# Softmax sums and reciprocals turned on VectorE instead of TensorE, and other begins for the blocks of powers

## The chip, the cores and the metric

The kernel runs on one core of a Trainium2 chip. The metric is device time in microseconds (us), the median of several executions; lower is better. TensorE is PE in the profile (PEld its weight loads), VectorE DVE, ScalarE ACT, GpSimd POOL, and SyncE, which issues most DMAs, SP.

## The reference

Two heads are computed and concatenated along the last axis. All data is float32, L = 2048, D = 448.

```
# A: a convolution with a state-space kernel (S4D), 448 channels, 256 states
dt = exp(log_dt);  A = -exp(log_A_real) + 1j*A_imag;  C = (C_real + 1j*C_imag)*dt
P  = exp(A*dt * pos)                       # (448, 256, 2048): powers of one number per channel and state
K  = 2*real(einsum("dn,dnl->dl", C, P))
y  = irfft(rfft(u, 2L)*rfft(K, 2L))[:L] + u*D_skip
# B: full attention, 16 heads of 28
q, k, v = heads(x @ wqkv);  p = softmax(q k^T * 28**-0.5);  out = (p v) @ wo
```

## The kernel before

One program does both heads, interleaved by hand. A first stage (to about 230 us) projects x to q, k and v and makes the seeds of the powers. Then comes the attention loop, and beside it, in slots, everything of head A.

**The attention loop** (lines 1061-1118) has 256 steps: 16 units u (4 groups g of 4 heads, times 4 chunks c of 512 queries), each of 16 steps over 128 keys. A step issues its work in the order written out in ORDER (line 35): four scores matmuls s0-s3 (s_mm, line 769: PE writes pss, ACT takes the exponential into p), four matmuls m0-m3 for the row maxima of the unit after next to come (max_mm, line 189: PE writes a bank of the ring pm; for m0 ACT takes a relu into rl, for m1 DVE adds and reduces with a custom instruction, for m2 and m3 DVE reduces), the product with v (pv, pv_step, line 776: eight column-tiled matmuls into po), up to three power products on DVE (v: vec, line 1056), the planning of blocks of powers (k), and two slots (f). After step 236 there are no more maxima, and a step has a third slot. In this part of the program every engine keeps the order in which the program issues (KEPT, line 89), so an instruction that waits holds up all that stands behind it on its engine.

**The ring.** w_tile (line 127) hands out three PSUM banks pm0-pm2 in turn. The maxima's matmuls and all slot work use it; a matmul into a bank waits until the last reader of that bank is done.

**Slots.** slot (line 1012) runs at most one thing: first what is urgent and due (soon_slot, line 1005: kept with a number of the slot from which it is due), then output projections (p_due), then matmuls of the powers (m_due), then u parts (u_due), then spectrum and finish tasks of head A (f_slot). UG (line 41) says after how many slots the maxima's end, the sums and the scaling are due. After the last step a loop (line 1122) runs slots until all is done.

**The end of a unit** (fin, line 789). The product with v has v's 28 columns and a column of ones for each head in 32 partitions, so po holds for each of four heads 28 rows of output and in row 28 the sum of the softmax. fin copies po to o (ACT). Two slots later *sums* takes a ring bank and multiplies, with o as the weights, by a constant sel (one column per head that picks row 28): 16 small products, in 32 instructions, whose output has queries on partitions. DVE takes the reciprocal of these 16 columns, ACT spreads each over 32 columns (rb). Another two slots later *scale* multiplies rb by the identity, again in 32 instructions, so that each reciprocal stands in the 32 rows of its head, and DVE multiplies o by that (on). on goes to DRAM, or, for the last group, into four output projections (project, line 815), each due from two steps after fin on, one more for each step.

**Blocks of powers.** 56 blocks b of eight channels. A block's e half (nine POOL instructions, e_power, line 689) and g half (DVE, g_powers, line 703) are begun by k_begin (line 1032); before that k_seed (line 1027) has made its two seeds, one per step, in tiles with two buffers each:

```python
def k_seed(s_):
    b = k_due[0] if k_due else NB
    if b < NB and b not in egs and done["mm"] >= b - 2 and K0 + b * KP <= s_ + (1 if b in es else 2):
        k_seeds(b)
```

KP is 3.5: block b is not begun before step 3.5 b. Its matmuls (k_mm, line 730) are due in slots KD = 4, 5 and 6 steps after the begin: two products of e and g, the second of which sets done["mm"] = b, and a fold with w. k_start (line 685) copies the factors into PSUM (zg) on ACT at the begin.

**Head A besides.** u parts (lines 622-667) run in steps 3 to about 102; spectrum tasks (line 831) from step 195 on, finish tasks (line 874) from about 233 on; the first finish job also loads the constant wb (line 895).

Of the kernel before, what the change touches and what calls it, by code (L numbers as in the profile page):

```python
# [8 lines left out]
F32 = mybir.dt.float32  # L9
F32R = mybir.dt.float32r  # L10
I32 = mybir.dt.int32
AF = mybir.ActivationFunctionType
# [6 lines left out]
D = 448  # L19

H = 16
DH = 28
G = 4
HG = H // G
CQ = 512
NQ = L // CQ
NK = L // 128
# [13 lines left out]
UG = (2, 2, 4)  # L41
PS = 1
SGB, XB, XL = 2, 5, 4
K0, KP, KD, UP = 0, 3.5, 4, 3
A0, A1 = 26, 31

N1 = 32
N2 = 64
# [3 lines left out]
NB = D // 8  # L52
# [40 lines left out]
def body(ctx, tc, a, out):  # L93
    nc = Engines(tc)
# [22 lines left out]
    const = pool(ctx, "const")  # L117
    ident = const.tile([128, 128], F32, name="ident")
    nc.sync.dma_start(ident, a["ident"])
    sel = const.tile([128, HG], F32, name="sel")  # L120
    kones = const.tile([128, 1], F32, name="kones")
    w1 = const.tile([128, 2, 128], F32, name="w1")

# [3 lines left out]
    def w_tile():  # L127

        n_ring[0] += 1
        return ps_w[0].tile([128, CQ], F32, name=f"pm{n_ring[0] % ps_w[1]}")  # L130
# [7 lines left out]
    def mm32(o, w, x_, start, stop, at=0):  # L138

        for i in range(w.shape[-1] // 32):  # L140
            c = slice(32 * i, 32 * i + 32)
            nc.tensor.matmul(o[c], w[:, c], x_, start=start, stop=stop, tile_position=(0, at + 32 * i))
# [85 lines left out]
    with ExitStack() as st:  # L228
# [32 lines left out]
        t = a["A_log_dt"]  # L261
# [56 lines left out]
        pw2 = s_p.tile([128, LV], F32, name="pw2")  # L318
        nc.sync.dma_start(pw2, a["pw2"])
        nc.sync.dma_start(kones, a["kones"])  # L320
        nc.sync.dma_start(sel, a["sel"])
        nc.sync.dma_start(w1, a["w1"])
        def split_w(s):
            for k in range(NCK):
# [285 lines left out]
    kq_p = pool(kq_st, "kq_p")  # L610
# [58 lines left out]
    sds, egs = {}, {}  # L669
# [58 lines left out]
    uts, zgs, es = {}, {}, {}  # L728
# [60 lines left out]
    def fin(u, s_):  # L789
        g, c = divmod(u, NQ)  # L790
        o = kq_p.tile([128, CQ], F32, name="o")
        nc.scalar.activation(o, o_u[u], AF.Copy)
        on = kq_p.tile([128, CQ], F32, name="on", bufs=2)
        rb = kq_p.tile([128, 4, HG, 32], F32, name="rb")
        og = og_u.pop(u, None)

        def sums():
            pw = w_tile()
            for t in range(4):
                mm32(pw[:, t * HG:(t + 1) * HG], o[:, t * 128:(t + 1) * 128], sel, start=True, stop=True)  # L800
            r = kq_p.tile([128, 4, HG], F32, name="r", bufs=2)
            nc.vector.reciprocal(r, pw[:, :4 * HG].rearrange("p (t h) -> p t h", h=HG))
            nc.scalar.activation(rb, r[:, :, :, None].to_broadcast([128, 4, HG, 32]), AF.Copy)

        def scale():
            pw = w_tile()
            for t in range(4):
                mm32(pw[:, t * 128:(t + 1) * 128], rb[:, t].rearrange("p h e -> p (h e)"), ident, True, True)
            nc.vector.tensor_tensor(on, o, pw, ALU.mult)
            if g < G - 1:  # L810
                nc.sync.dma_start(on_d[c][g], on)
            else:
                p_due.extend((s_ + PD + PS * t, lambda t=t: project(t)) for t in range(4))

        def project(t):
            pw = w_tile()
            ts = slice(t * 128, (t + 1) * 128)
            for g2 in range(G):
                mm32(pw[:, :D], og[:, g2, ts] if g2 < G - 1 else on[:, ts], wo_t[g2 // 2][:, g2 % 2, :],
                     start=g2 == 0, stop=g2 == G - 1)  # L820
            y = kq_p.tile([128, D], F32, name="y", bufs=2)
            nc.scalar.activation(y, pw[:, :D], AF.Copy)
            q0 = c * CQ + t * 128
            nc.sync.dma_start(out[q0:q0 + 128, D:], y)

        soon_slot(UG[1], sums)
        soon_slot(UG[2], scale)

    fk = {}

# [43 lines left out]
    def finish(f, qc, p, ps, bufs=(2, 2)):  # L874

        t_ = {}

        def rows(t, m, i, n):

            w = t.ap[0][0]  # L880
            return bass.AP(tensor=t.tensor, offset=t.offset + (16 * m + 4 * qc + i) * w + f * DF,
                           ap=[[32 * w, 64], [w, n], [1, DF]])

        def load():
            t_["zi"] = p.tile([128, 4, 2, DF], F32, name="zi", bufs=bufs[0])
            nc.sync.dma_start(t_["zi"], z_d[f].rearrange("(q m h c) k d -> (h c k) q m d", m=2, h=2, c=2)
                              [:, qc * 4:qc * 4 + 4])
            t_["u"] = p.tile([128, 4, DF], F32, name="ut", bufs=2)
            for m in range(2):
                nc.sync.dma_start(t_["u"][64 * m:64 * m + 64], rows(u_a, m, 0, 4))  # L890
            if "dsk" not in fk:
                fk["dsk"], fk["wb"] = p.tile([128, D], F32, name="dsk"), p.tile([128, 64], F32, name="wb")
                t = a["A_D_skip"]
                nc.sync.dma_start(fk["dsk"], bass.AP(tensor=t.tensor, offset=t.offset, ap=[[0, 128], [1, D]]))
                nc.sync.dma_start(fk["wb"], a["wb"])

        def skip():
            nc.gpsimd.tensor_tensor(t_["u"], t_["u"],
                                    fk["dsk"][:, None, f * DF:(f + 1) * DF].to_broadcast([128, 4, DF]), ALU.mult)

        def one(i):
            if i == 0:
                t_["ot"] = p.tile([128, 4, DF], F32, name="ot", bufs=bufs[1])
            pf = ps()[:, :DF]
            for m in range(2):
                mm32(pf[64 * m:64 * m + 64, :], fk["wb"], t_["zi"][:, i, m, :], True, True, 64 * m)
            ot = t_["ot"]
            jbi = lambda t, o_: t.rearrange(o_ + " -> p j b i", j=4, i=2)
            nc.vector.tensor_tensor(jbi(ot[:, i], "p (j b i)"), jbi(pf, "p (b j i)"), jbi(t_["u"][:, i], "p (j b i)"), ALU.add)
            if i % 2:  # L910
                for m in range(2):
                    nc.sync.dma_start(rows(out, m, i - 1, 2), ot[64 * m:64 * m + 64, i - 1:i + 1])
        return load, [(0, lambda i=i: one(i)) for i in range(4)], skip
# [11 lines left out]
    k_seeds(0)  # L925
    k_seeds(0)

    urgent, back = collections.deque(), collections.deque()
    powers = {"g": collections.deque(), "e": collections.deque()}
    done = {"mm": -1}  # L930
    u_jobs = [u_stage1(q) for q in range(16)] + [u_stage2(m) for m in range(16)]
# [17 lines left out]
    u_due = collections.deque((3 + UP * i + (UP / 2) * c + (4 if i > 15 else 0), i, c) for i in range(32) for c in range(2))  # L949
    k_due = collections.deque(range(NB))  # L950
    m_due = collections.deque()
# [3 lines left out]
    f_tasks = {k: collections.deque() for k in "sf"}  # L955
    f_loaded = {k: collections.deque() for k in "sf"}
    s_done = [0]
    n_slot, f_next = [0], {"s": 0, "f": 0}
# [46 lines left out]
    def soon_slot(gap, f):  # L1005
        n_urgent[0] += 1
        urgent.append((n_slot[0] + gap, n_urgent[0], f))
        q = sorted(urgent)
        urgent.clear()
        urgent.extend(q)  # L1010

    def slot(s_):
        n_slot[0] += 1
        if urgent and urgent[0][0] <= n_slot[0]:
            urgent.popleft()[2]()
        elif s_ >= NS and f_slot(s_, "s"):
            pass
        elif p_due and p_due[0][0] <= s_:
            p_due.popleft()[1]()
        elif m_due and m_due[0][0] <= s_:  # L1020
            m_due.popleft()[1]()
        elif u_due and u_due[0][0] <= s_:
            u_part(*u_due.popleft()[1:])
        else:
            f_slot(s_, "s") or f_slot(s_, "f")

    def k_seed(s_):
        b = k_due[0] if k_due else NB
        if b < NB and b not in egs and done["mm"] >= b - 2 and K0 + b * KP <= s_ + (1 if b in es else 2):
            k_seeds(b)  # L1030

    def k_begin(s_):
        if not (k_due and K0 + k_due[0] * KP <= s_ and k_due[0] in egs and not powers["e"] and not powers["g"]):
            return
        b = k_due.popleft()
        k_start(b)
        powers["g"] += g_powers(b)
        powers["e"] += [lambda i=i, q=q: e_power(b, i, q) for i in range(3) for q in range(3)]
        p0, p1, p2 = k_mm(b)

        def m1():
            p1()
            done["mm"] = b
        m_due.extend((s_ + KD + i, t_) for i, t_ in enumerate((p0, m1, p2)))
        last[0] = b
# [73 lines left out]
    pv_step(*prev)  # L1119
    fin(prev[0], NS)  # L1120
    s = NS
    while urgent or p_due or m_due or u_due or any(q[k] for q in (f_jobs, f_tasks, f_loaded) for k in "sf"):
        slot(s)
        s += 0.5
    assert not k_due and not powers["g"] and not powers["e"]
# [4 lines left out]
def constants():  # L1130
    import numpy as np
    k = {}
    k["ident"] = np.eye(128)
    sel, ones = np.zeros((128, HG)), np.zeros((128, 1))
    for j in range(HG):
        sel[32 * j + DH, j] = 1.0
        ones[32 * j + DH:32 * j + DH + 2] = 1.0
    k["sel"], k["kones"] = sel, ones
    k["pw2"] = np.tile(2.0 ** np.arange(LV), (128, 1))
    n1, k1 = np.arange(N1), np.arange(N1)  # L1140
    n2, k2 = np.arange(N2), np.arange(N2)
# [43 lines left out]
```

## Time and profile before

| what | time |
|---|---|
| median of 3 runs | 1278.66 us (1276.97 to 1278.9) |
| the profiled execution | 1278.83 us |
| its span, first to last instruction | 1277.0 us |
| PE busy | 1216.2 us (95%) |
| ACT busy | 967.0 us (76%) |
| DVE busy | 922.6 us (72%) |
| POOL busy | 843.6 us (66%) |

A row of the profile that begins with L77 names line 77, the helper through which every instruction is issued, so groups are told apart by their tiles, written out<-in. After the tiles come the shapes, the count, then the busy time in us and the mean of one in ns, then the engine's idle time before them with what ended it. A row of a stretch is its begin and end, its length, then the busy time of each engine with the number of its instructions, the granted clock of PE, the DMA engines' busy share and GB/s. A row of the timeline is start, length, engine, instruction, and idle time before it in brackets. Ends of matmuls are modelled, so several of them overlap in the rows; what a piece of PE's work costs is better read from the starts of what follows, or from whole steps.

### The profile page before, as it was taken

Reading aid. Unit: us, or ns where it says so; the run is one execution under the profiler, and the core shown is the slowest. Engines: PE = TensorE matmul, PEld = TensorE weight load, DVE = VectorE, ACT = ScalarE, POOL = GpSimd, SP = SyncE. Lnnn points to the kernel's source line nnn. Section 1 sums busy time; section 2 is a strip of 40 time slices with the busy share of each in tenths; the row PEclk is TensorE's granted clock in tenths of the full one; section 3 lists DMA queues with packets and bytes.
Section 4 is the critical chain, followed back from the end, with each engine's and each line's share of the span. In section 5 each row is a group of like instructions: output and inputs, shape, how many; then the busy total and the mean of one; then the engine's idle time right before and its main releaser. Section 6 shows DMA issues by size and latency. Waiting matters only on the chain.

```text
span 1277.0 us, 33251 instructions
## 1 busy us (share of the span) xinstructions
PE 1216.2 (95%) x12593; PEld 692.5 (54%) x12593; DVE 922.6 (72%) x2106; ACT 967.0 (76%) x2162; POOL 843.6 (66%) x728
## 2 busy tenths in 40 slices
PE   6788888999999999999999999999999999999998
PEld 4666764555555555555555555555555555544433
DVE  5788966877777877778778988888887645645111
ACT  5888865788888888888888888888887656656552
POOL 2666740798788888878689999989995222324321
PEclk9999898899999999999999999999999999999999
DMA  6678789436554645475533133432224533657656
GB/s 194 211 258 290 275 278 359 124 88 187 159 154 114 169 118 159 123 224 177 171 101 96 57 80 105 145 91 71 83 60 149 171 139 135 205 162 237 203 163 174
DMA packets 203528, 206.22 MB, mean 161 GB/s; under 512 B 98344, under 2 KB 162408, under 8 KB 201320
## 3 DMA queue, kind: packets, MB, share of 16 engines
q1 hardware_dynamic: 202840, 203.50, 51.8%
q8 instruction: 99, 1.62, 0.5%
q10 hardware_dynamic: 528, 0.59, 0.2%
q14 instruction: 61, 0.50, 0.1%
HBM read 121.60 MB, written 82.18 MB: 160 GB/s over the span
## 4 chain that ended last, share of the span: by engine, by line
PE 79%; DVE 9%; ACT 5%; issue 3%; POOL 2%; DMA 1%; SPq 1%; ACTq 0%; POOLq 0%; DVEq 0%
PE pm L77 44%; PE pss L77 17%; PE po L77 17%; DVE tri L77 1%; ACT tri L77 1%; DVE mx L77 1%; DVE sg L77 1%; SPq L77 1%; ACT rl L77 1%; DVE hl L77 1%; DVE px L77 1%; ACT p L77 1%; PE pt L77 1%; POOL p L77 1%; DVE g L77 1%
## 5 line engine op out<-in xcount | busy, mean ns | idle before, releaser
L77 ACT ACTIVATE p<-pss 128x512 f32<-128x512 f32 x1024 | 561.3, 611 | 111.5 <-PE pss L77 108.4
L77 PE MATMUL pss<-qhat,khat 128*128 128x512 f32 x1024 | 402.8, 399 | 1.5 <-ACT p L77 1.4
L77 DVE TENSOR_REDUCE mx<-pm 128x1 f32<-128x512 f32 x480 | 308.3, 683 | 108.9 <-PE pm L77 106.8
L77 PE MATMUL pm<-khat,qhat 128*128 128x512 f32 x749 | 326.3, 439 | 6.6 <-ACT rl L77 4.4
L77 POOL TENSOR_TENSOR e<-e,sdb 128x256 f32<-128x256 f32 x168 | 201.8, 1201 | 111.4 <-ACT e L77 62.2
L77 PE MATMUL po<-p,v 128*32 128x512 f32 x2048 | 269.1, 594 | 0.0
L77 POOL TENSOR_TENSOR e<-e,eu 128x256 f32<-128x256 f32 x168 | 248.1, 1477 | 13.2
L77 PEld LDWEIGHTS pm<-khat,qhat 128*128 128x128 f32 x749 | 141.2, 189 | 202.8 <-ACT p L77 46.9
L77 DVE CUSTOM_DVE_ANT_0 rl<-pm,rl 128x512 f32<-128x512 f32 x259 | 178.2, 688 | 73.7 <-ACT rl L77 70.8
L77 PEld LDWEIGHTS pss<-qhat,khat 128*128 128x128 f32 x1024 | 190.4, 188 | 46.1 <-issue 10.8
L77 POOL TENSOR_TENSOR eu<-e,sdb 128x256 f32<-128x256 f32 x168 | 201.9, 1202 | 0.0
L77 POOL TENSOR_TENSOR p<-pr,pr 64x448 f32<-64x448 f32 x64 | 73.1, 1142 | 161.4 <-PE pm L77 134.7
L77 ACT ACTIVATE rl<-pm 128x512 f32<-128x512 f32 x259 | 156.8, 607 | 15.4 <-PE pm L77 9.4
L77 DVE TENSOR_TENSOR g<-g,zg 128x128 f32<-128x128 f32 x392 | 161.9, 413 | 3.4
L77 PE MATMUL pm<-kdif,qhat 128*128 128x512 f32 x249 | 100.9, 405 | 6.0 <-DVE xn L77 4.1
L77 PE MATMUL pm<-xh,khat 128*128 128x512 f32 x256 | 85.0, 423 | 12.1 <-DVE hl L77 5.3
L77 DVE TENSOR_TENSOR zg<-g,zg 128x128 f32<-128x128 f32 x224 | 88.0, 393 | 5.0
L77 PEld LDWEIGHTS pm<-e,g 128*32 128x32 f32 x3584 | 57.2, 109 | 43.9 <-issue 16.2
L77 DVE TENSOR_TENSOR pr<-pm,ub 128x448 f32<-128x448 f32 x64 | 37.0, 619 | 56.4 <-PE pm L77 42.0
L77 PE MATMUL pm<-e,g 128*32 128x64 f32 x3584 | 73.0, 222 | 1.9 <-POOL e L77 1.3
L77 ACT ACTIVATE y<-pm 128x448 f32<-128x448 f32 x48 | 26.5, 553 | 58.2 <-PE pm L77 35.9
L77 ACT ACTIVATE ub<-pm 128x224 f32<-128x224 f32 (+1 forms) x96 | 38.7, 448 | 39.5 <-PE pm L77 37.4
(135 smaller groups left out, 1436.7 us busy)
## 6 DMA issues: line engine op xcount, KB each, us to landing
sdb<-sd SPq DMA_DIRECT2D x55, 336.0 KB
qhat<-q SPq DMA_DIRECT2D x64, 256.0 KB
khat<-k SPq DMA_DIRECT2D x64, 256.0 KB
sd<-sg SPq DMA_DIRECT2D x8, 1456.0 KB
k<-hl SPq DMA_DIRECT2D x16, 512.0 KB
mw<-in_mw SPq DMA_DIRECT2D x16, 512.0 KB
sd<-qhat SPq DMA_DIRECT2D x8, 896.0 KB
yu_d<-ub SPq DMA_DIRECT2D x64, 112.0 KB
```

The lines of the kernel that those rows point to most:

```text
L77: i = f(*args, **kw)
```

## The change

The sums' and the scaling's matmuls go, and with them sel and ACT's spreading copy. *sums* now turns o on DVE in blocks of 32x32 (SBUF to SBUF, 128x512), so that column 28 of each block holds the sums with queries on partitions; DVE takes the reciprocal of these 16 columns. *scale* turns the reciprocals, each read 32 times, into a ring bank, again on DVE, and multiplies as before. Both leave the slots: they stand in a queue of their own, *free*, with the same number of slots to wait, and slot runs whatever of it is due and then one thing as before. The condition of k_seed and k_begin on the step is now a table K_BEGIN: 10/3 steps per block up to block 33, then 3.75 from step 113.5 on; the rest of both conditions is as it was. The constant wb is loaded at the start, in sel's place, and no longer by the first finish job.

```diff
-K0, KP, KD, UP = 0, 3.5, 4, 3
+KD, UP = 4, 3
+K_BEGIN = [b * 10 / 3 if b < 34 else 112 + (b - 33.6) * 3.75 for b in range(56)]
...
-    sel = const.tile([128, HG], F32, name="sel")
+    wb = const.tile([128, N2], F32, name="wb")
...
         on = kq_p.tile([128, CQ], F32, name="on", bufs=2)
-        rb = kq_p.tile([128, 4, HG, 32], F32, name="rb")
         og = og_u.pop(u, None)
+        t_ = {}
 
         def sums():
-            pw = w_tile()
-            for t in range(4):
-                mm32(pw[:, t * HG:(t + 1) * HG], o[:, t * 128:(t + 1) * 128], sel, start=True, stop=True)
-            r = kq_p.tile([128, 4, HG], F32, name="r", bufs=2)
-            nc.vector.reciprocal(r, pw[:, :4 * HG].rearrange("p (t h) -> p t h", h=HG))
-            nc.scalar.activation(rb, r[:, :, :, None].to_broadcast([128, 4, HG, 32]), AF.Copy)
+            t = kq_p.tile([128, NK, 32], F32, name="rb")
+            nc.vector.transpose(t.rearrange("p b e -> p (b e)"), o)
+            t_["r"] = kq_p.tile([128, NK], F32, name="r", bufs=2)
+            nc.vector.reciprocal(t_["r"], t[:, :, DH])
 
         def scale():
             pw = w_tile()
-            for t in range(4):
-                mm32(pw[:, t * 128:(t + 1) * 128], rb[:, t].rearrange("p h e -> p (h e)"), ident, True, True)
+            nc.vector.transpose(pw.rearrange("p (b e) -> p b e", e=32), t_["r"][:, :, None].to_broadcast([128, NK, 32]))
             nc.vector.tensor_tensor(on, o, pw, ALU.mult)
...
-        soon_slot(UG[1], sums)
-        soon_slot(UG[2], scale)
+        free.append((n_slot[0] + UG[1], sums))
+        free.append((n_slot[0] + UG[2], scale))
...
     def slot(s_):
         n_slot[0] += 1
+        while free and free[0][0] <= n_slot[0]:
+            free.popleft()[1]()
         if urgent and urgent[0][0] <= n_slot[0]:
...
-        if b < NB and b not in egs and done["mm"] >= b - 2 and K0 + b * KP <= s_ + (1 if b in es else 2):
+        if b < NB and b not in egs and done["mm"] >= b - 2 and K_BEGIN[b] <= s_ + (1 if b in es else 2):
...
-        if not (k_due and K0 + k_due[0] * KP <= s_ and k_due[0] in egs and not powers["e"] and not powers["g"]):
+        if not (k_due and K_BEGIN[k_due[0]] <= s_ and k_due[0] in egs and not powers["e"] and not powers["g"]):
```

More of the change, by code (lines that the diff above doesn't have):

```diff
@@ L320, in body @@
         nc.sync.dma_start(kones, a["kones"])
-        nc.sync.dma_start(sel, a["sel"])
+        nc.sync.dma_start(wb, a["wb"])
         nc.sync.dma_start(w1, a["w1"])
@@ L891, in load @@
             if "dsk" not in fk:
-                fk["dsk"], fk["wb"] = p.tile([128, D], F32, name="dsk"), p.tile([128, 64], F32, name="wb")
+                fk["dsk"] = p.tile([128, D], F32, name="dsk")
                 t = a["A_D_skip"]
                 nc.sync.dma_start(fk["dsk"], bass.AP(tensor=t.tensor, offset=t.offset, ap=[[0, 128], [1, D]]))
-                nc.sync.dma_start(fk["wb"], a["wb"])
         def skip():
@@ L905, in one @@
             for m in range(2):
-                mm32(pf[64 * m:64 * m + 64, :], fk["wb"], t_["zi"][:, i, m, :], True, True, 64 * m)
+                mm32(pf[64 * m:64 * m + 64, :], wb, t_["zi"][:, i, m, :], True, True, 64 * m)
             ot = t_["ot"]
@@ L926, in body @@
     k_seeds(0)
-    urgent, back = collections.deque(), collections.deque()
+    urgent, free = collections.deque(), collections.deque()
     powers = {"g": collections.deque(), "e": collections.deque()}
@@ L1121, in body @@
     s = NS
-    while urgent or p_due or m_due or u_due or any(q[k] for q in (f_jobs, f_tasks, f_loaded) for k in "sf"):
+    while urgent or free or p_due or m_due or u_due or any(q[k] for q in (f_jobs, f_tasks, f_loaded) for k in "sf"):
         slot(s)
@@ L1133, in constants @@
     k["ident"] = np.eye(128)
-    sel, ones = np.zeros((128, HG)), np.zeros((128, 1))
+    ones = np.zeros((128, 1))
     for j in range(HG):
-        sel[32 * j + DH, j] = 1.0
         ones[32 * j + DH:32 * j + DH + 2] = 1.0
-    k["sel"], k["kones"] = sel, ones
+    k["kones"] = ones
     k["pw2"] = np.tile(2.0 ** np.arange(LV), (128, 1))
```

## The prediction

> **What bounds the kernel now.** I read the page first: the span, then the chain that ended last.
>
> ```profile
> span 1277.0 us, 33251 instructions
> ...
> PE 79%; DVE 9%; ACT 5%; issue 3%; POOL 2%; DMA 1%; SPq 1%; ACTq 0%; POOLq 0%; DVEq 0%
> PE pm L77 44%; PE pss L77 17%; PE po L77 17%; DVE tri L77 1%; ACT tri L77 1%; DVE mx L77 1%; DVE sg L77 1%; SPq L77 1%; ACT rl L77 1%; DVE hl L77 1%; DVE px L77 1%; ACT p L77 1%; PE pt L77 1%; POOL p L77 1%; DVE g L77 1%
> ```
>
> The chain is PE, above all PE writing pm, the ring of three banks. Next I cut the attention at the first scores matmul (pss) of a step: steps 0-100 (with the u jobs), 101-192 (powers only), 193-236, and from 237.
>
> ```profile
> core 0: us, PE busy (x) PEld busy (x) DVE busy (x) ACT busy (x) POOL busy (x), PEclk, DMA share, GB/s
> 230.54:634.07 403.53, 402.04 (x4728) 219.59 (x4726) 317.29 (x751) 337.12 (x779) 333.44 (x261) 1.00 0.53 151
> 634.07:963.69 329.62, 326.67 (x3904) 185.86 (x3902) 286.51 (x686) 278.55 (x632) 303.63 (x241) 1.00 0.31 86
> 963.69:1167.55 203.86, 203.05 (x2099) 108.16 (x2097) 121.66 (x253) 132.72 (x263) 65.21 (x53) 1.00 0.52 171
> 1167.55:1277.03 109.48, 99.21 (x1118) 40.66 (x1116) 22.35 (x51) 52.86 (x100) 32.13 (x24) 0.99 0.64 189
> ```
>
> PE is busy almost all of the first three stretches, at a granted clock of 1.00. The reader should look at the third busy column too: DVE has 86 us free in the first stretch (403.5 less 317.3), but only 43 in the second (87% busy). POOL, 92% busy there, has the powers' e half; it bounds nothing as long as the steps there don't get shorter, and by the sum below they don't. So what leaves PE is worth its full time only where DVE can take what it gets. Single steps show what PE's pieces cost:
>
> ```profile
> 899.99:903.02 3.03, 3.03 (x17) 1.58 (x16) 2.71 (x7) 2.44 (x7) 2.87 (x3) 1.00 0.93 229
> 842.90:846.39 3.49, 3.49 (x49) 2.02 (x48) 3.39 (x10) 2.97 (x8) 3.41 (x3) 1.00 0.00 0
> 625.58:629.82 4.24, 4.24 (x57) 2.28 (x56) 3.42 (x10) 3.37 (x9) 3.54 (x3) 1.00 0.62 221
> 849.86:853.18 3.32, 3.32 (x49) 1.85 (x48) 2.99 (x9) 3.04 (x8) 3.16 (x3) 1.00 0.49 106
> 682.15:686.52 4.37, 4.37 (x81) 3.05 (x80) 3.84 (x9) 3.08 (x8) 4.29 (x3) 1.00 0.18 67
> 735.26:739.37 4.11, 4.04 (x65) 2.29 (x64) 3.52 (x10) 3.83 (x9) 3.95 (x5) 1.00 0.02 4
> 294.27:298.40 4.13, 4.03 (x66) 2.29 (x65) 3.55 (x10) 3.84 (x9) 3.91 (x5) 1.00 0.15 62
> 616.57:620.90 4.33, 4.01 (x65) 2.29 (x64) 3.91 (x10) 3.78 (x9) 4.09 (x6) 1.00 0.88 284
> ```
>
> In order: a step with empty slots 3.03 us; with one product of the powers (e,g) 3.49, so a product is 0.46; with product and u part 4.24, so a u part is 0.75; with the sums alone 3.32, so **the sums are 0.29**; with the spread of the reciprocals and a product 4.37, so **the spread is 0.88**. In the last three the sums stand beside a fold of powers, which I take as a product: parts of 3.78, so they hold 0.33, 0.35 and 0.55 of waiting, 1.2 in all. PE is a sum of parts.
>
> **The change, part by part.** The groups with shapes kept apart give what goes and what stays:
>
> ```profile
> L77 PE MATMUL pm<-ident,rb 128*32 128x128 f32 x512 | 17.3, 275 | 0.6 <-ACT rb L77 0.6
> L77 PE MATMUL pm<-sel,o 128*32 128x4 f32 x512 | 7.0, 175 | 0.3 <-ACT o L77 0.3
> L77 ACT ACTIVATE rb<-r 128x512 f32<-128x512 f32 x16 | 10.1, 630 | 4.9 <-DVE r L77 4.9
> L77 DVE RECIPROCAL r<-pm 128x16 f32<-128x16 f32 x16 | 4.0, 251 | 0.3 <-PE pm L77 0.3
> L77 DVE TENSOR_TENSOR on<-o,pm 128x512 f32<-128x512 f32 x16 | 10.9, 682 | 2.3 <-PE pm L77 2.1
> L77 DVE TENSOR_TENSOR g<-g,zg 128x256 f32<-128x256 f32 x224 | 92.3, 412 | 1.5
> L77 DVE TENSOR_TENSOR g<-g,zg 128x512 f32<-128x512 f32 x56 | 38.2, 681 | 0.0
> ```
>
> *Off PE:* per unit 32 sums and 32 spread instructions (512/16 each), 0.29 + 0.88 = 1.17 us; 16 units. *Off ACT:* 0.63 per unit, not on the chain; I cost it at nothing. *On to DVE:* two turns of 128x512 per unit. No row shows a turn. From 256 to 512 columns a g product goes from 412 to 681 ns, 1.05 ns a column over a base of 0.14 us. At one column a step a turn is 0.68; at two, 0.14 + 0.27 = 0.41; at half a column, 1.22. I take **0.69**, nearest to the 128x512 rows, and keep 0.41 and 1.22 for the range. DVE gets 16 x 1.38 = 22 us. The reciprocal (0.25) and the scaling (0.68) stay; the reciprocal now waits for DVE's own turn instead of PE.
>
> [...]
>
> **What a turn delays.** DVE keeps program order. The turns stand behind m1's custom maximum and ahead of the reduces of m2 and m3. The new waits themselves are short: the first turn waits for ACT's copy of o, issued a step before; the second for a ring bank that DVE itself read last. But whatever waits behind them on DVE waits longer, and PE waits for that. One late step:
>
> ```profile
> 744.53 0.49 PEld L77 LDWEIGHTS pm<-e,g 128*32 128x32 f32 x32 [0.36 <-DVE g L77]
> 745.07 0.68 DVE L77 CUSTOM_DVE_ANT_0 rl<-pm,rl 128x512 f32<-128x512 f32 x1
> 745.68 0.41 DVE L77 TENSOR_TENSOR g<-g,zg 128x256 f32<-128x256 f32 x1
> 746.13 0.43 DVE L77 TENSOR_TENSOR zg<-g,zg 128x256 f32<-128x256 f32 x1
> 746.51 1.29 DVE L77 TENSOR_REDUCE mx<-pm 128x1 f32<-128x512 f32 x2
> 747.47 0.39 PE L77 MATMUL pm<-khat,qhat 128*128 128x512 f32 x1
> ```
>
> The matmul at 747.47 is the next m1; three banks on, it reuses the bank that the first reduce frees (746.51 + 1.29/2 = 747.16). The room is 0.3; I take 0.2 for the handover's sake. This step has one product in its slots; a second slot with a u part adds 0.75 of room (0.95), empty slots take 0.46 (none left). No power product ahead adds 0.84 (0.41 + 0.43); the 128x512 one takes 0.27 (0.68 less 0.41). What exceeds the room is a stall on PE. The sums queue a turn and the reciprocal, 0.94; the scaling a turn and the product, 1.38.
>
> By the planner's rules, with the two moved out of the slots, the units meet these steps (sums/scaling, stall in us). Steps 17/18: 0/0. 33/34 (two slots; one slot behind the big product): 0/1.45. 49/50: 0.94/0.43. 65/66: 0.94/0.43. 81/82: 0/0.43. 97/98 (its slots empty): 0.26/1.38. Together 6.3. Steps 113/114: 0.74/1.38. 129/130 (no power ahead): 0.74/0.34. 145/146: 0.74/1.38. 161/162 and 177/178: 0.94/1.18 each. Together 9.6. The rate is not invented: the maxima's transposed end queues 0.2 + 0.56 us on DVE at such a place, and the second of these pairs (same slots, without it) is 0.54 shorter:
>
> ```profile
> 777.99:785.66 7.67, 7.47 (x98) 3.94 (x97) 7.42 (x21) 5.93 (x14) 7.15 (x6) 1.00 0.02 4
> 828.26:835.39 7.13, 7.13 (x98) 4.07 (x96) 6.74 (x18) 5.90 (x14) 6.70 (x5) 1.00 0.35 116
> ```
>
> **The blocks' begin.** I cost it at nothing, for a reason in the code: k_seed takes block b only when the product of block b-2 is done (b-2's begin + 5 steps); its two seeds need two steps, and k_begin comes before k_seed, so the block begins 7 steps after b-2. That is one per 3.5 steps, whatever K_BEGIN allows sooner; and 3.75 from block 34 on only catches up with 3.5 b at b = 56. The trace has this rhythm (copies at the begin of blocks 37, 38 and 39, steps 130, 133, 137):
>
> ```profile
> 742.74 0.29 ACT L77 ACTIVATE zg<-sdb 128x144 f32<-128x144 f32 x1
> 753.42 0.29 ACT L77 ACTIVATE zg<-sdb 128x144 f32<-128x144 f32 x1 [0.58 <-DVE g L77]
> 766.52 0.36 ACT L77 ACTIVATE zg<-sdb 128x144 f32<-128x144 f32 x1
> ```
>
> The wb load moves into sel's place on SP's queue, one issue for one, and leaves the finish job: nothing. What each freed slot takes instead (u parts, then spectrum tasks) only comes earlier.
>
> **The end.** After the last step the chain is copy, sums, reciprocal, spread, scaling, then four projections:
>
> ```profile
> 1254.40 0.60 ACT L77 ACTIVATE o<-po 128x512 f32<-128x512 f32 x1 [1.14 <-PE po L77]
> 1257.43 2.44 PE L77 MATMUL pm<-ua,og 128*32 128x448 f32 x24
> 1259.69 0.94 PE L77 MATMUL pm<-ua,on 128*32 128x448 f32 x8
> 1260.44 0.56 PE L77 MATMUL pm<-zi,wb 128*32 128x224 f32 x8
> ```
>
> Afterwards copy to 1255.0, turn, reciprocal, turn, product (0.69 + 0.25 + 0.69 + 0.68): `on` at 1257.3. The first projection's og part needs no PE work ahead of it, runs meanwhile, and ends at about 1257.4, so its on part ends at 1258.3 instead of 1260.6: 2.3 off. Slots freed at 209-241 also bring three finish tasks (zi) ahead of the end, some 0.3 each net: 0.9. Together 3.2.
>
> **Sum, against the profiled execution** (1278.83, 1.8 over its span; the median of the runs is 1278.66). Steps 17-98: PE -6 x 1.17 = -7.0, two waits -0.9, stalls +6.3: -1.6. Steps 113-178: -5.9, one wait -0.3, stalls +9.6: +3.4. Steps 193/194: -1.2, and about as much back, since a spectrum product falls beside the scaling: 0. Units at 209, 225, 240: -3.5, +0.9 where two spectrum tasks stand beside the sums: -2.6. End: -3.2. Together -4.0: **1274.8 us**.
>
> **The rivals.** (1) *DVE's idle time takes the turns*: 43 us free in the tight stretch speak for it, the 0.54 above against. With no stalls all of -1.17 x 15 - 1.2 - 3.2 = -22 would stay, 1257; with a turn of 0.41, some 20 exposed turns x 0.28 = 5.6 more than forecast, 1269. Taken as 1266. (2) *Slower: the turn runs at half a column a step.* Then each exposed turn costs 0.53 more, 22 x 0.53 = 11.7: 1286.5. It decides from a turn of about 0.9 us (0.69 + 4.0/20). Against it: every 128x512 row on DVE is at 0.68-0.69; for it: no row turns anything, and none turns 4-byte data into PSUM. [...] (3) *The begins do move*: DVE's powers in steps 113-192 thin out by 3.5/3.75, and a third of those stalls goes: -4 more, 1271. Against: the gate above.
>
> **How the numbers follow.** Forecast (1271-1278) 0.47, rival 1 0.22, rival 2 0.25, rival 3 0.06. About 0.2% (2.6 us) is what a measurement tells from no change, so the forecast's own range splits, 0.27 faster and 0.2 same; with rivals 1 and 3 faster has 0.55, same 0.20, slower 0.25. The range 1264 to 1287 takes in both ends of the turn.
>
> **What would show it.** Turn rows on DVE: near 690 ns right, near 1200 wrong. Scaling steps of 3.5 to 4.9 us instead of 4.37, waits of PE on mx; a longer stretch from step 113 to 193, a shorter one from 17 to 113; the begin copies still 7 steps apart by twos. If PE waits on mx no more than before, rival 1; if PE's steps lengthen by both turns in full, rival 2.

## The result, and the profile after

| | median us | runs | against before, 95% interval |
|---|---|---|---|
| before | 1278.22 | 20 (1276.9 to 1279.6) | |
| after | 1280.5 | 20 (1279.2 to 1281.65) | 1.0018 [1.0012, 1.0024] |

The change makes the kernel 2.3 us slower; 4.0 faster was forecast. The profiled execution of after took 1280.06 us, its span is 1.2 longer than that of before. First the page of after: the span, and the chain that ended last (shares of the span by engine).

```profile
span 1278.2 us, 31211 instructions
...
PE 72%; DVE 12%; ACT 5%; POOL 5%; issue 3%; DMA 2%; SPq 0%; ACTq 0%; POOLq 0%; DVEq 0%
```

PE's share went from 79% to 72%, as 1024 matmuls left it; DVE has 12% of the chain where it had 9, and POOL 5 where it had 2. So the end is now set more often by something that PE waits for. The turns themselves have these rows (busy us, mean ns of one):

```profile
L78 DVE STREAM_TRANSPOSE pm<-r 128x512 f32<-128x512 f32 x16 | 11.5, 720 | 0.0
L78 DVE STREAM_TRANSPOSE rb<-o 128x512 f32<-128x512 f32 x16 | 11.3, 705 | 1.1 <-ACT o L78 1.1
L78 DVE RECIPROCAL r<-rb 128x16 f32<-128x16 f32 x16 | 4.1, 254 | 0.6
```

They cost 0.71 and 0.72 us, so that price is as forecast. Then the same cuts as in the prediction, at the first scores matmul of a step: steps 17-112, 113-192, 193-208, 209-236, and from 237. Of each stretch its ends, its length, then PE, PEld, DVE, ACT and POOL busy, and PE's granted clock. Before, then after:

```profile
294.27:678.24 383.97, 380.68 (x4543) 209.28 (x4542) 301.74 (x715) 320.48 (x745) 313.27 (x247) 1.00 0.53 152
678.24:963.69 285.45, 284.43 (x3447) 162.51 (x3445) 250.10 (x600) 241.77 (x548) 267.27 (x212) 1.00 0.30 86
963.69:1030.18 66.49, 65.71 (x738) 37.24 (x737) 45.18 (x97) 48.31 (x98) 25.67 (x20) 1.00 0.52 172
1030.18:1167.55 137.37, 137.33 (x1362) 70.92 (x1360) 76.48 (x157) 84.41 (x166) 39.54 (x33) 1.00 0.52 170
1167.55:1277.00 109.45, 99.21 (x1118) 40.66 (x1116) 22.35 (x51) 52.86 (x100) 32.13 (x24) 0.99 0.64 189
```

```profile
293.11:675.80 382.69, 374.96 (x4159) 201.18 (x4158) 309.32 (x727) 317.86 (x739) 313.23 (x247) 1.00 0.53 152
675.80:961.61 285.81, 280.07 (x3126) 154.72 (x3125) 256.07 (x610) 239.62 (x543) 267.30 (x212) 1.00 0.30 86
961.61:1037.12 75.51, 67.34 (x674) 36.22 (x673) 46.50 (x99) 48.06 (x97) 25.65 (x20) 0.95 0.45 151
1037.12:1174.43 137.31, 137.23 (x1273) 69.76 (x1272) 79.20 (x161) 84.12 (x166) 40.87 (x34) 1.00 0.55 175
1174.43:1278.20 103.77, 94.40 (x950) 37.95 (x948) 25.00 (x55) 50.14 (x96) 30.79 (x22) 1.00 0.65 192
```

Read the lengths: -1.3, +0.4, **+9.0**, -0.1, -5.7. Ahead of step 17 lie -1.2, which the change doesn't explain: in e2 and e2b below, which issue the same up to step 195, step 17 begins at 292.8 and 294.2, so this part varies by itself. Between the same two runs one step of the first stretch (65) differs by 1.16 us, so a single trace does not settle a difference as small as the first two. One stretch loses all that the others gain, and in it nearly all is one step, 197: from 4.33 us to 12.80. The waits of PE in after, grouped (us in total, times, the longest):

```profile
...
PE pm L78 <- POOL e L78: 8.8, 4, 6.5
...
PE pm L78 <- DVE mx L78: 7.0, 20, 1.1
...
PE pm L78 <- DVE on L78: 4.4, 10, 0.7
```

Of these before had

```profile
PE pm L77 <- DVE mx L77: 3.4, 12, 1.1
```

and none on `on`. So PE does wait for DVE more than before; but the longest wait is not one on DVE. It is on POOL's `e`, the e half of the last block's powers. POOL's instructions from then on, first before, then after:

```profile
963.59 1.30 POOL L77 TENSOR_TENSOR e<-e,eu 128x512 f32<-128x512 f32 x1
964.97 1.91 POOL L77 TENSOR_TENSOR e<-e,sdb 128x1024 f32<-128x1024 f32 x1
...
968.83 2.40 POOL L77 TENSOR_TENSOR e<-e,eu 128x1024 f32<-128x1024 f32 x1
980.11 4.80 POOL L77 TENSOR_TENSOR p<-pr,pr 64x448 f32<-64x448 f32 x4 [8.88 <-PE pm L77]
```

```profile
961.56 1.30 POOL L78 TENSOR_TENSOR e<-e,eu 128x512 f32<-128x512 f32 x1
975.54 4.76 POOL L78 TENSOR_TENSOR p<-pr,pr 64x448 f32<-64x448 f32 x4 [12.69 <-DVE pr L78]
980.38 1.91 POOL L78 TENSOR_TENSOR e<-e,sdb 128x1024 f32<-128x1024 f32 x1
...
984.23 2.32 POOL L78 TENSOR_TENSOR e<-e,eu 128x1024 f32<-128x1024 f32 x1
```

The order is another. `p<-pr,pr` are the four instructions of the first spectrum task's two joins (join, line 852 of after). Before, the scaling held a slot of step 194, so the task's first part ran at step 195 and its second, which calls the joins, at 196. Block 55 begins at step 193, and its powers are handed to POOL three at a time at the place 'k' of steps 193, 194 and 195, so all nine stood ahead of the joins. After, the slot is free, each part runs one step sooner, and the second stands in a slot of step 195, ahead of that step's 'k'. POOL keeps program order and runs far ahead of PE here: it is done with the sixth power at 962.86 and then sits at the joins for 12.69 us, until PE has reached step 195 and DVE has made `pr`, the products that the joins add and subtract. Behind them are three powers (6.2 us) that waited for nothing else. PE needs them in step 197:

```profile
979.52 0.40 PE L78 MATMUL pm<-khat,qhat 128*128 128x512 f32 x1
986.61 1.08 PE L78 MATMUL pm<-e,g 128*32 128x64 f32 x32 [6.46 <-POOL e L78]
```

And the step costs more than its wait of 6.5. Step 197 cut at the wait, with the granted clock behind the busy times:

```profile
979.92:986.61 6.69, 0.23 (x2) 0.01 (x1) 0.70 (x2) 1.50 (x4) 6.47 (x4) 0.80 0.00 0
986.61:988.50 1.89, 1.89 (x40) 1.23 (x44) 0.00 (x0) 0.22 (x1) 0.00 (x0) 0.50 0.00 0
988.50:990.30 1.80, 1.80 (x22) 0.60 (x14) 0.00 (x0) 0.00 (x0) 0.00 (x0) 0.50 0.00 0
```

Of the first row's 6.69 us PE is idle for 6.46. Its granted clock falls to 0.50 in this wait (at 983.99) and is back at 1.00 at 990.81, so PE works at half its clock for 4.2 us. Before, the same 56 matmuls took 2.20 us (981.64 to 983.84) at 1.00, 2.0 less. 6.5 and 2 are the 8.5 that the step grew by.

### The profile page after: what moved, and what is told of

It reads as the page before. It is cut to its first block, busy times and chain, and to the rows that moved or that the text cites. A ratio compares the mean times of both kernels' runs of the same rounds, so it can differ in the third digit from the quotient of the medians.

```text
span 1278.2 us, 31211 instructions
## 1 busy us (share of the span) xinstructions
PE 1201.0 (94%) x11569; PEld 671.0 (52%) x11569; DVE 942.8 (74%) x2138; ACT 959.0 (75%) x2146; POOL 843.7 (66%) x728
## 4 chain that ended last, share of the span: by engine, by line
PE 72%; DVE 12%; ACT 5%; POOL 5%; issue 3%; DMA 2%; SPq 0%; ACTq 0%; POOLq 0%; DVEq 0%
PE pm L78 41%; PE pss L78 15%; PE po L78 15%; DVE mx L78 2%; DVE tri L78 2%; ACT rl L78 1%; ACT p L78 1%; POOL qhat L78 1%; DVE rl L78 1%; POOL p L78 1%; POOL e L78 1%; DVE g L78 1%; ACT tri L78 1%; DVE zg L78 1%; DMA xn<-in_B_x 1%
## 5 line engine op out<-in xcount | busy, mean ns | idle before, releaser
L78 PEld LDWEIGHTS pss<-qhat,khat 128*128 128x128 f32 x1024 | 190.5, 188 | 45.6 <-issue 11.4
```

The source lines that it names most:

```text
L78: i = f(*args, **kw)
```

## The experiments

**Theory (POOL's order):** the freed slot puts the joins ahead of block 55's last powers; that is +8.5 to 9, and without it the change is a gain. **Rival A:** the turns make DVE late, and POOL and PE only wait for that. **Rival B:** the early spectrum task collides by its own work. The table K_BEGIN needs no run: with 3.5 b in its place the changed kernel issues the same instructions in the same order on all five engines, and the old kernel with the new table issues its old ones. It changes nothing, as the gate in k_seed said.

Before, timed again beside each of them, took 1278.3 to 1278.7. e6b and e9 do not compute the scaling's values; the others compute the whole.

| run | median us | against before, 95% interval | step 197, us |
|---|---|---|---|
| e1 joins behind the powers | 1271.17 | 0.9945 [0.9932, 0.9957] | 4.24 |
| e2 PE's sums, no slot taken | 1288.39 | 1.0075 [1.0063, 1.0088] | 12.95 |
| e2b the same, joins behind | 1279.1 | 1.0008 [0.9999, 1.0016] | 4.25 |
| e3 turns in slots | 1274.38 | 0.9967 [0.9955, 0.9979] | 4.33 |
| e5 e1, second turn twice | 1283.84 | 1.0043 [1.0030, 1.0057] | 4.23 |
| e6b e1, no turns, product from SBUF | 1269.48 | 0.9936 [0.9923, 0.9948] | 4.25 |
| e7 e1, turns at the step's end | 1284.24 | 1.0046 [1.0033, 1.0059] | 4.24 |
| e8 e1, first turn twice | 1280.1 | 1.0015 [1.0006, 1.0024] | 4.24 |
| e9 e1, no turns, product from PSUM | 1266.06 | 0.9903 [0.9890, 0.9917] | 4.23 |
| e10 e1, projections later | 1274.97 | 0.9975 [0.9966, 0.9985] | 4.24 |
| e11 e1, second turn into SBUF | 1277.94 | 0.9996 [0.9987, 1.0005] | 4.24 |
| e12 e1, scaling a step later | 1274.46 | 0.9969 [0.9957, 0.9982] | 4.26 |

**e1: the joins behind the powers.**

```diff
         def last():
             forth(1)
-            join(0)
-            join(1)
+            if powers["e"]:
+                powers["e"].extend([lambda: join(0), lambda: join(1)])
+            else:
+                join(0)
+                join(1)
```

> The changed kernel, with one thing more: where block 55 still has powers to run, the two joins (POOL p<-pr,pr) are put behind them, so that POOL's order is again powers, then joins. Nothing else moves. Theory (POOL's order): step 197, which took 12.79 us where 4.33 was before, comes back to about 4.3-4.6, and the 8.5 us are gone: 1280.5 - 8.5 = 1272. Rival A (DVE's load: the turns make the spectrum products and maxima late, POOL only waits for them): step 197 stays long and the time stays at 1279-1281. Rival B (the spectrum task is early in itself: its PE work or loads collide there): the time moves by under 3 us.

1271.2, and step 197 is 4.24. POOL in e1, with step 197 as a stretch below it:

```profile
962.03 1.30 POOL L78 TENSOR_TENSOR e<-e,eu 128x512 f32<-128x512 f32 x1
963.41 1.91 POOL L78 TENSOR_TENSOR e<-e,sdb 128x1024 f32<-128x1024 f32 x1
...
976.23 4.80 POOL L78 TENSOR_TENSOR p<-pr,pr 64x448 f32<-64x448 f32 x4 [6.59 <-DVE pr L78]
```

```profile
979.98:984.22 4.24, 4.24 (x66) 2.55 (x64) 1.99 (x5) 3.22 (x8) 1.05 (x1) 1.00 0.00 0
```

The joins begin no sooner than in after (976.2 against 975.5): it mattered only what stood behind them. The granted clock stays at 1.00. Every other stretch is that of after within 0.15 us, so the order of two pieces of work on POOL is worth 8.5 at step 197, and 9.3 between the medians. Rival B falls with it: the spectrum task is as early as in after. e1 is faster than both kernels, and no later run was faster that computes the whole.

**e2 and e2b: the freed slots without the turns.** The kernel before with the queue *free* added, PE's sums and spread called from it; e2b has e1's edit too.

```diff
-        soon_slot(UG[1], sums)
-        soon_slot(UG[2], scale)
+        free.append((n_slot[0] + UG[1], sums))
+        free.append((n_slot[0] + UG[2], scale))
```

> The kernel before, sums and spread still on PE and ACT, but called beside the slots instead of in them, so that the slots are free as in the changed kernel. No turn on DVE. Theory (POOL's order): the freed slot of steps 193 and 194 alone brings the spectrum's join ahead of block 55's last powers; a stall of about 8.5 us at step 197, and 1278.2 + 8.5 - about 1 (finish tasks taken ahead of the end) = about 1286. Rival A (the turns on DVE): no long step 197, 1277-1279.

> As the run before it, and the joins put behind block 55's powers. Theory (POOL's order): the stall goes, and what is left is the worth of the free slots alone, -0.9 for three finish tasks ahead of the end and nothing for the u parts: 1277.3. With it the turns themselves are the difference of the changed kernel with joins behind (1272) from this one, about -5. Rival A: no difference from the run before it.

POOL in e2:

```profile
962.98 1.30 POOL L77 TENSOR_TENSOR e<-e,eu 128x512 f32<-128x512 f32 x1
977.84 4.77 POOL L77 TENSOR_TENSOR p<-pr,pr 64x448 f32<-64x448 f32 x4 [13.56 <-DVE pr L77]
982.69 1.91 POOL L77 TENSOR_TENSOR e<-e,sdb 128x1024 f32<-128x1024 f32 x1
```

The stall is there with no turn in the kernel, and goes with the joins behind. Rival A falls for step 197. e2 is 9.8 slower than before where 7.8 was expected. e2b also prices the free slots, with sums and spread on PE: nothing, where 0.9 was expected. Between e2b and e1 only the turns differ, and where wb is loaded: 1279.1 to 1271.2, **-7.9 us** for sums and spread on DVE instead of PE and ACT.

**e3: the turns take slots again.** The two lines of e2, the other way round, in after.

> The changed kernel, its two turns on DVE called from the slots again as the sums were before, so that no slot is freed. Theory (POOL's order): the spectrum's first join is again behind block 55's powers, step 197 is about 4.3, and the time is 1272-1273 (the end without the finish tasks ahead of it is 0.9 later than with free slots). Rival A (the turns make DVE late): 1280 or more, since the turns are all there.

Faster than before and than after, with all turns in it; step 197 is 4.33, and rival A falls here too. The turns are worth 4.2 with the slots taken (e3 against before), 7.9 with the slots free (e1 against e2b): the two halves of the change do not simply add up.

e3 is 3.2 slower than e1 where 0.9 was expected. Its profiled execution is the slowest of its six (1276.81), and in it 4.1 of the 4.6 us between the two spans lie from step 255 on. There the last unit's first turn (1253.23) stands behind an addition of a finish task, for which DVE waits 7.90 us for POOL. So PE waits longer for the product, 2.00 us against 0.62 in e1, and the granted clock is 0.61 from 1257.19 to 1261.15. It is the same kind of loss as at step 197: something ready stands behind something that waits. How much of it the other five executions have is not shown.

**e5, e8, e9, e6b: what a turn costs.** Beside e1, one turn doubled (e5 the second, e8 the first):

```diff
+            nc.vector.transpose(pw.rearrange("p (b e) -> p b e", e=32), t_["r"][:, :, None].to_broadcast([128, NK, 32]))
             nc.vector.transpose(pw.rearrange("p (b e) -> p b e", e=32), t_["r"][:, :, None].to_broadcast([128, NK, 32]))
```

or both left out (e9: the reciprocal of a tile of ones, and ACT copies o into the bank that the product reads):

```diff
-            nc.vector.transpose(t.rearrange("p b e -> p (b e)"), o)
-            nc.vector.reciprocal(t_["r"], t[:, :, DH])
+            nc.vector.reciprocal(t_["r"], ones)
...
-            nc.vector.transpose(pw.rearrange("p (b e) -> p b e", e=32), t_["r"][:, :, None].to_broadcast([128, NK, 32]))
+            nc.scalar.activation(pw, o, AF.Copy)
```

> The changed kernel with the joins behind (1271.2), and the second turn of each unit, from the reciprocals into PSUM, done twice. It prices one more turn (0.72) at the place of the second one. Theory (room on DVE: past some tenths of a us what stands in front of the maxima's reduces is a stall of PE): at the ten scaling steps from 34 to 178 that are already longer the whole 0.72 comes on top, and once at the end; 11 x 0.72 = 7.9: 1279. Rival (DVE's idle time takes a turn): only the one at the end, 1272.

> The changed kernel with the joins behind, and both turns left out: 16 strided columns of o plus 1 stand for the reciprocals, and the scaling multiplies by them spread in its own access. The attention's scaling is therefore not computed; the lone product and the small operation stay on DVE, the ring keeps its rotation. It gives what the turns cost in all. Theory (room on DVE): the measured stalls of the changed kernel, some 10 us between steps 17 and 178, lose most of themselves, and the end is 1.4 shorter: 1262. Rival (idle time takes the turns): 1.4 at the end alone: 1269.8.

> The changed kernel with the joins behind (1271.2), and the first turn of each unit, o into rb, done twice. The second turn done twice cost 0.72-0.78 at every unit, also from step 209 on, where DVE is idle for 40% of the time; there the product of the scaling holds a bank of the ring, and the projection stands right behind it. The first turn holds no bank. Theory (a turn costs PE its time where PE waits for its bank or its product; a turn that only stands in front of the reduces is hidden in part): nothing from step 209 on but 0.7 at the end, and about 0.35 at each of 11 steps before: 4.5, so 1275.7. Rival (any DVE time at these places comes on top in full): 11 x 0.7 + 0.7 and more, 1280-1282.

> The changed kernel with the joins behind, without the two turns: the reciprocal reads a constant tile, and ACT copies o into the ring bank where the second turn wrote, so the scaling's values are not computed. The reciprocal (0.25) and the product out of PSUM (0.69) stay as they are, which the first try at this did not keep (its lone product read two SBUF operands and took up to 1.95 us). Theory (both turns are on the path at most units): 10 scaling steps x 0.72, three projections x 0.72, the end 1.4 and about 2 at the sums' steps: 13 less, 1258. Rival (the turns lie in idle time and only their doubling passes it): 1.4 at the end and 2.2 at the projections, 1267.5.

e6b says little: its product reads two SBUF operands and takes 1.24 us in the mean instead of 0.69 (more under e11). The other three belong together. Without both turns, 16 x 1.43 = 22.8 us of DVE, the kernel is 5.1 us faster (e1 less e9; the intervals leave about 2 us to such a difference). That is the price of DVE's time, not the whole price of the turns: in e9 ACT's copy and the product hold the scaling's bank for 1.36 us (848.18 to 849.54 at step 162), about as long as turn and product do in after (853.51 to 854.95). PE's waits for `mx` are 3.6 us in e9, about those of before, and 7.1 in e1.

One turn more, 16 x 0.71 = 11.4 us, costs 8.9 (e8) or 12.7 (e5). So the theory in the form of e9's expectation, 13, is wrong, and its rival, 3.7, is nearer. For the doubling it is the other way round: the rival's 1272 for e5 is wrong, the theory's 1279 and 1275.7 are too low by 4.8 and 4.4, and e8 comes out where its rival had it. I read this as idle time that takes the first turns and has nothing left for another. Where it is used up, a step of after shows (unit 10's sums at step 161 and scaling at 162; stretches of before, then of after):

```profile
849.86:853.18 3.32, 3.32 (x49) 1.85 (x48) 2.99 (x9) 3.04 (x8) 3.16 (x3) 1.00 0.49 106
853.18:857.80 4.62, 4.62 (x81) 3.05 (x80) 4.17 (x12) 3.16 (x8) 4.54 (x3) 1.00 0.82 253
```

```profile
847.10:850.17 3.07, 3.07 (x18) 1.59 (x16) 2.71 (x8) 2.25 (x5) 2.91 (x3) 1.00 0.48 107
850.17:855.80 5.63, 4.11 (x49) 1.98 (x48) 5.53 (x15) 3.50 (x9) 5.22 (x3) 1.00 0.79 257
```

```profile
849.35 0.70 DVE L78 STREAM_TRANSPOSE rb<-o 128x512 f32<-128x512 f32 x1
...
850.53 1.27 DVE L78 TENSOR_REDUCE mx<-pm 128x1 f32<-128x512 f32 x2
...
851.26 0.50 PE L78 MATMUL pm<-khat,qhat 128*128 128x512 f32 x1 [0.70 <-DVE mx L78]
...
853.51 0.72 DVE L78 STREAM_TRANSPOSE pm<-r 128x512 f32<-128x512 f32 x1
...
854.26 0.69 DVE L78 TENSOR_TENSOR on<-o,pm 128x512 f32<-128x512 f32 x1
855.00 0.50 PE L78 MATMUL pm<-khat,qhat 128*128 128x512 f32 x1 [0.25 <-DVE on L78]
```

The sums' step has no wait: 3.07, next to an empty step's 3.03. DVE comes out of it late, its last reduces run in the next step, and PE pays there, first for the reduces (0.70 at 851.26), then, behind 0.57 for ACT's `rl`, for the product (0.25 at 855.00): the scaling holds one of three ring banks until `on` is done, and PE is back at that bank with the second of the maxima behind it. With one more turn all of it is at that place: 0.72 to 0.79 at each of ten scaling steps from 34 to 178 in e5. In e8 it depends on the unit: 0.73 to 0.76 at steps 50, 66, 114, 130, 146 and 178, 0.56 at 98, 1.69 at 162, but 0.30 at 34 and 0.03 at 82, though the added turn stands in the step ahead and holds no bank. So lateness that DVE carries over is a cause by itself; in e5 the bank is also held longer, and the two are not separated there. From step 209 on, DVE is free 40% of the time, and e5 still pays 0.76 at step 210. There it is another wait, in e5:

```profile
1044.60 1.48 DVE L78 STREAM_TRANSPOSE pm<-r 128x512 f32<-128x512 f32 x2
...
1046.85 0.96 PE L78 MATMUL pm<-ua,on 128*32 128x448 f32 x8 [0.74 <-DVE on L78]
```

With the scaling out of the slots, the first projection stands in the very slot behind it and waits for its product.

**e10: the projections a step later.** `PD + (u < NU - 1)` for PD in project's due time.

> The changed kernel with the joins behind, and the projections of units 12 to 14 due one step later. With the slots freed, the first projection stands in the same slot as the scaling, and PE waits 0.78 for its product (steps 210, 226, 242). Theory: those three waits go, 2.3, if nothing else falls due later for it: 1269. Rival (a projection moved to a later step only moves the wait to the end, where the last tasks are): 1271 or more.

A miss: 3.8 slower than e1. Step 210 falls from 6.52 to 3.34 and step 226 by 2.3, but steps 214 and 230 take it back, and from step 237 on it is 2.5 longer: the work was only moved, as the rival has it.

**e7: another place on DVE.** The queue beside the slots is run at the end of a step, not at a slot.

```diff
-        while free and free[0][0] <= n_slot[0]:
+        while s_ >= NS and free and free[0][0] <= n_slot[0]:
             free.popleft()[1]()
...
+        while free and free[0][0] <= n_slot[0] + 1:
+            free.popleft()[1]()
         if sm < NS and sm % NK == NK - 1:
```

> The changed kernel with the joins behind, and the two turns issued on DVE at the end of a step, behind the reduces of m2 and m3 and ahead of the next step's m1, instead of between m1 and the reduces. Theory (room on DVE, and where the queue is short): the reduces are not held up, and m1's custom maximum waits for ACT anyway (0.26 each in the mean): about 0.3 less at each of some 18 steps, 1266-1268. Rival (it is DVE's whole load in the step that counts, not the place): 1271.

13 slower: the wrong way for the theory, and against the rival too, since the place matters. Steps 113 and 114 are 1.2 longer each. At the step's end the turn stands ahead of the next step's m1 maximum, and the scaling's bank has fallen in between the maxima; which of the two does it was not separated.

**e11: the second turn into SBUF.** No ring bank is held.

```diff
-            pw = w_tile()
-            nc.vector.transpose(pw.rearrange("p (b e) -> p b e", e=32), t_["r"][:, :, None].to_broadcast([128, NK, 32]))
-            nc.vector.tensor_tensor(on, o, pw, ALU.mult)
+            t = kq_p.tile([128, NK, 32], F32, name="rb")
+            nc.vector.transpose(t, t_["r"][:, :, None].to_broadcast([128, NK, 32]))
+            nc.vector.tensor_tensor(on, o, t.rearrange("p b e -> p (b e)"), ALU.mult)
```

> The changed kernel with the joins behind, and the second turn into SBUF instead of a ring bank. The scaling then holds no bank, so PE does not wait for its product in the ring; but the product reads two SBUF operands, as the one that took 0.68 to 1.95 us and ended with POOL's instruction. Theory (the bank held is what PE waits for): scaling steps 0.3-0.7 shorter at ten steps, 1265-1268. Rival (the product waits for POOL, 0.5 us longer in the mean, and the reduces behind it too): 1273-1277.

Slower by 6.8: the rival, and a little more than its range. The scaling's steps did become shorter, 34 by 1.24, 146 by 0.96, but the next ones grew by more: 35 by 1.88, 163 by 3.82. The product takes longer. Its rows (least, median and longest ns of 16), in e1 and in e11:

```profile
L78 DVE TENSOR_TENSOR on<-o,pm x16: 686/686/689, 300.2 to 1253.6; 128x512 f32<-128x512 f32 x16
```

```profile
L78 DVE TENSOR_TENSOR on<-o,rb x16: 691/1180/2141, 300.2 to 1259.0; 128x512 f32<-128x512 f32 x16
```

**e12: the scaling a step later.** `UG[2] + 2` for units 0 to 11, so that a step lies between backlog and scaling.

> The changed kernel with the joins behind (1271.2), and the scaling of units 0 to 11 one step later, so that a step lies between the sums' turn and the scaling. What the traces show: in the step of the sums DVE falls behind by the first turn without PE waiting (the last reduce ends 1.2 to 1.6 us into the next step instead of 0.56), and the scaling's step pays it all, since PE needs the ring bank that the scaling holds until its product is done. Theory (a backlog carried into the scaling): the step between takes most of the backlog, some 0.4-0.5 at each of eight units: 4 less, 1267. Rival (the second turn and the product, 1.41 together, are what PE waits for, wherever they stand): 1271, the stall only moves a step.

Nearer the rival, though 3.3 slower than e1, where it expected no difference: steps 34, 114 and 146 fall by 0.9 to 1.25, and the steps behind them grow by 0.6 to 1.2. The stall goes with the scaling.

Beside e11 this says more. At all eleven scaling steps from 18 to 178 the lengths in e11 and e12 agree within 0.06 us (4.49 in both at 162, where e1 has 5.64). So a scaling that holds no bank costs its own step as little as one that isn't there. What PE pays there in e1 beyond e11, 0.18 to 1.24 us, is the held bank. DVE's time comes back a step later: in e11 nine of the eleven next steps grow by 0.66 to 3.82, the longer product included. What is left of the stall at the scaling's step I put down to the step ahead; no run takes it out alone.

## Why the prediction was wrong

The step that failed is half a sentence: "What each freed slot takes instead (u parts, then spectrum tasks) only comes earlier." With it went the term "Steps 193/194: -1.2, and about as much back, since a spectrum product falls beside the scaling: 0"; the stretch of steps 193-208 grew by 9.0. The sentence holds for PE; but a task is also moved past POOL's queue, and the joins came out ahead of three powers. That POOL "bounds nothing" was said of steps 101-192; behind them the prediction didn't ask. These rows of before were enough to work it out:

```profile
974.95 1.15 DVE L77 TENSOR_TENSOR pr<-pm,ub 128x448 f32<-128x448 f32 x2 [0.64 <-PE pm L77]
...
981.64 0.65 PE L77 MATMUL pm<-e,g 128*32 128x64 f32 x32
```

POOL ran the powers in question at 964.97-971.2, ten microseconds ahead of need. With its slot one step sooner, the task's second part makes its `pr` where the first part's stood, until 976.1. Joins 4.8, powers 6.2: the block's product can't begin before 987.1, and PE is there at 981.64. That is a stall of 5.5; measured were 6.46. The drop of the clock behind it, 2 more, no row of before shows.

The other steps, against after (e1 where step 197 would hide it):

- *Sums 0.29, spread 0.88 off PE:* right. Step 161 is 3.07, an empty step with the sums gone. Steps 210 and 226 of e3, whose slots hold what those of before hold, are 0.85 and 0.88 shorter.
- *A turn at 0.69:* right, 0.705 and 0.720. Rival 2, half a column a step, is out: its turn would have taken 1.22.
- *Stalls 6.3 in steps 17-98:* the stretch 17-112 is -1.3 where -1.6 was forecast; by the same sum 6.6 were put back. That this is near is in part luck, as the next lines show. *Stalls 9.6 in steps 113-178:* +0.4 measured, +3.4 forecast, so 6.6 were put back.
- *Where the stalls lie:* the sum gave each step its own room and charged the sums' steps 6.2 in all; they hold 0.4 (e1, by the prediction's prices of the parts). At the scaling's steps it charged 9.6; by difference they took some 13. At 161/162 it is 0 for 0.94 and 1.89 (5.63 less (4.62 - 0.88)) for 1.18. DVE carries its lateness across the step, and PE meets it one step later, together with the held bank.
- *Rival 1, idle time takes the turns:* in e9's measure 17.7 of the 22.8 us of turns cost nothing. But its sign, that PE waits on `mx` no more than before, failed (7.0 for 3.4), and its -22 isn't there even with no turn at all: e9 is 12.6 under before. The bank held by copy and product may hold the rest; that was not tried by itself.
- *The begins:* right; no instruction moves, as said above of K_BEGIN.
- *The end and the units from 209 on, -5.8 together:* -0.1 and -5.7. The sum is right. The place is another because tasks move from the end into earlier steps: in e2b, with the slots free and no turn, the two are +1.6 and -2.2 against before.

In e1 the sum of the stretches from step 17 on is -5.7, and the medians give -7.4; the forecast of -4.0 was on the side of too little, and step 197 turned its sign. The part ahead of step 17, some 1 us in either trace, stays unexplained.

## What to carry to other kernels

A planner that hands work out to slots fixes the order on every engine; when a slot comes free, write down the new order on each queue that the moved task touches, and ask of each whether something that could run now stands behind something that waits. An engine that is far ahead of the bound, as POOL was by ten microseconds, hides that until one instruction ties it to the bound. And room on an engine is a stock, not a price: here 1.43 us of DVE a unit cost 0.3, the next 0.7 cost 0.6 to 0.8; double a suspect before believing that it is free. A buffer of a short ring that an instruction holds is a second price, beside the engine's time: here 0.18 to 1.24 us at a scaling step (e1 against e11).

## What the runs showed of the hardware

One long wait of PE cost more than itself. Ahead of the product in step 197 of after PE was idle for 6.46 us; the granted clock fell from 1.00 to 0.50 when 3.84 us of them had passed (at 983.99) and was back at 1.00 after 4.20 us of work (at 990.81). That work took 2.20 us at 1.00 in before, so the drop cost about 2 us on top of 6.5.

A DVE product whose two operands lie in SBUF took 691 to 2141 ns beside POOL, against 686 to 689 with one of them in PSUM (e11, e1). The longest in e11, with POOL's instruction that ran when it began:

```profile
740.49 1.91 POOL L78 TENSOR_TENSOR e<-e,sdb 128x1024 f32<-128x1024 f32 x1
```

```profile
740.81 2.14 DVE L78 TENSOR_TENSOR on<-o,rb 128x512 f32<-128x512 f32 x1
```

It ends 0.54 us behind POOL's, and so do all eleven that took longer than 0.7 us (0.54 to 0.55); the other five, which began with no instruction of POOL's that ran on for more than 0.05 us, took 691 to 694 ns. Why it takes longer beside POOL no row shows. In this kernel the turn into PSUM has with it a reason of its own, a product of 0.69 us in the mean instead of 1.18 (e1, e11), at the price of a ring bank.
